# Fewer, wider warm-up matmuls, and the sort matrices' second half moved ahead of the first scores, in an attention and expert-mixture kernel on one core

## The chip, the core and the metric

The kernel runs on one NeuronCore of one Trainium2 chip. The metric is the device time of one execution in microseconds (us). A profile of one execution stands beside it; its times are counted from the first instruction of the span. Engines are named as in the profile: PE is TensorE (matmuls), PEld its weight loads, DVE is VectorE, ACT is ScalarE, POOL is GpSimd, SP is SyncE (which issues DMAs).

## The reference

Four batches of eight heads, 768 tokens of 64 numbers. Eight blocks of 96 tokens are mixed by an 8x8 matrix per head, which five rounds of row and column normalisation make (a Sinkhorn iteration); then attention within each block; then a mixture of four experts over the 3072 resulting rows of 512.

```
P = sort_net
for _ in range(5):
    P = exp(P - max(P, -1))
    P = P / (sum(P, -1) + 1e-9)
    P = P / (sum(P, -2) + 1e-9)
k_sorted = einsum('bhij,bhjcd->bhicd', P, k_blocks)      # v likewise
scores = q_b @ k_sb.T / sqrt(64)                         # within a block of 96
x = softmax(scores) @ v_sb                               # -> rows [3072, 512]
p = domain_probs / (sum(domain_probs, -1) + 1e-9)
out = sum over e of p[:, e] * (relu(x @ w1[e]) @ w2[e])
```

## The kernel before

The order of the work on each engine is the order in which the program is written: no scheduler moves anything. Four batches follow each other; attention of a later batch is spread in small pieces between the expert matmuls of an earlier one, by a table of slots (`PLANS`). Batch 0 has nothing in front of it, so its attention is written out by hand as a head (lines 1365 to 1417), in half heads of queries and half sets of blocks, and the change lies there and in what comes before it.

Before the head, three things run beside each other. DMAs issued by POOL bring queries, keys, values and then weights (lines 147, 110, 134, 141). ACT and DVE go through the five rounds on the 32 sort matrices (`sn`, lines 283 to 300): an Exp on ACT (L284) and five or six small operations on DVE, each waiting for the last. And PE runs matmuls on a constant tile, whose results nobody reads, by `warm` (L260): 84 of them with a moving operand of 128 columns, then, behind the fifth Exp in the program's text, 48 transposes of the first half of the queries (`h_q`, L271, copied by ACT at L274) and 30 more. PE doesn't wait for the Exp here, but ACT's copies of the transposed queries stand behind it on ACT.

After the fifth round, L304 writes the matrices in fp16, repeated 16 times (`sn16`): the first half of the rows on DVE, the second half on POOL. `r_half(a)` (L316) transposes a half by four matmuls into `ps_R`; for the first half DVE builds from it the operand `PI0` of the mix (L327). `mix_half` (L495) mixes keys or values by matmuls, `mixed` (L506) copies the result out of PSUM (keys to `kT` by ACT, values by DVE), `h_s` (L550) makes scores from `kT` and transposed queries and ACT takes their Exp (L556), `h_w` (L522) transposes mixed values and DVE copies them (L527), `h_a` (L567) multiplies the Exp with the values and DVE divides (L580, L581, tile `xsl`), `h_x` (L598) transposes the result into `xT`, and `group0` (L679) is the first expert layer of expert 0.

The head begins like this; `psm` and `psa` are two pools of two PSUM buffers each, and a buffer is free again when its last reader is done. `ps_R` is one of the two of `psm`; `mk1` takes the buffer that `ps_R` had, and `mv1` is in turn behind `mk1` and `mk0` in that pool.

```
mk0 = mix_half("k", 0, 0, psm, 8)      # 8 matmuls of keep_warm (L481) first
mixed("k", 0, mk0, 0, 2, act)
mv0 = mix_half("v", 0, 0, psa)
mixed("v", 0, mv0, 0, 2, vec)
h_s(0, 0)
r_half(1)
mixed("k", 0, mk0, 2, 2, act)
vec(Rs..., Rv...)                      # L1372: Rs, both halves in fp16
```

`Rs` is read by POOL for the second `PI0` and, later, for the mixes of batches 1 to 3.

## Time and profile before

| | us |
|---|---|
| median of 3 runs | 359.47 |
| lowest, highest | 359.26, 360.56 |
| span of the profiled execution | 357.8 |
| its time outside the span | not listed; the median less the span is 1.67 |
| PE busy | 351.6 of the span |
| DVE, ACT, POOL busy | 276.2, 170.6, 133.6 |

The page gives busy time of each engine, the chain of work that ended last (followed back from the last instruction to what released each), groups of instructions by source line, and DMA queues. Matmuls are pipelined: one of 128 columns lasts 219 or 314 ns in the profile, while the starts of such matmuls are 56 or 107 ns apart, so the distance between starts tells what one costs. A wait is the idle time of an engine before an instruction, put down to what released it; "issue" is idle time in which it waited for nothing that the profile shows.

### The profile page before, as it was taken

The numbers are of one execution on the slowest core, as the hardware profiler recorded it, in microseconds if no ns is written. First come the engines' busy times: TensorE is split into PE (matmuls) and PEld (weight loads), VectorE is DVE, ScalarE is ACT, GpSimd is POOL, SyncE is SP. The second block draws the span as 40 slices with busy tenths as digits, with TensorE's granted clock in tenths as the row PEclk, the third lists the DMA queues.
The fourth block names the chain that finished last, engine by engine and source line by source line (L and its number), as shares of the span: only waits on it lengthen the run. The fifth ranks groups of instructions, "written<-read, shape, count | busy, mean of one in ns | idle before, by whom it ended". The sixth has DMA issues, their size and how long they took to land.

```text
span 357.8 us, 9498 instructions
## 1 busy us (share of the span) xinstructions
PE 351.6 (98%) x3949; PEld 306.3 (86%) x3949; DVE 276.2 (77%) x552; ACT 170.6 (48%) x303; POOL 133.6 (37%) x149
## 2 busy tenths in 40 slices
PE   8899999999999999999999999999999999999996
PEld 8686867888888888888899988888888888888886
DVE  5754797869889587868978988896678886588963
ACT  2554240442434535367947258830288611688201
POOL 8864010375122222000535318840058800188400
PEclk9999999999999999999999999999999999999999
DMA  8999999999999999935996420005200015100011
GB/s 114 207 205 228 216 210 198 209 163 165 201 154 160 188 152 170 194 74 73 168 201 90 102 78 0 2 2 108 102 29 2 3 39 138 61 0 2 2 73 46
DMA packets 72022, 40.51 MB, mean 113 GB/s; under 512 B 40614, under 2 KB 66732, under 8 KB 71980
## 3 DMA queue, kind: packets, MB, share of 16 engines
q0 software_dynamic: 36576, 19.93, 41.9%
q1 hardware_dynamic: 35260, 19.92, 28.5%
q8 instruction: 31, 0.51, 0.6%
q14 instruction: 11, 0.09, 0.1%
q10 hardware_dynamic: 144, 0.07, 0.1%
HBM read 42.13 MB, written 6.34 MB: 135 GB/s over the span
## 4 chain that ended last, share of the span: by engine, by line
PE 95%; DVE 2%; ACT 1%; DMA 0%; issue 0%; DVEq 0%
PE ps_h L790 18%; PE ps_Q L1264 18%; PE ps_p L774 12%; PE ps_X L1121 10%; PE ps_Z L1121 7%; PE ps_Q L1121 7%; PE ps_Z L1264 6%; PE ps_h L679 3%; PE ps_o L714 3%; PE ps_p L830 3%; PE ps_a L453 2%; PE ps_s L418 2%; PE ps_k L399 1%; PE ps_v L365 1%; PE ps_a L567 1%; PE ps_mk L495 1%
## 5 line engine op out<-in xcount | busy, mean ns | idle before, releaser
L790 PE MATMUL ps_h<-xT,w 128*128 128x256 f16 x576 | 67.5, 273 | 0.0
L790 PEld LDWEIGHTS <-w 128*128 128x128 f16 x576 | 55.2, 98 | 7.2
L796 DVE SCALAR_TENSOR_TENSOR Hb<-ps_h,pb 128x1024 f16<-128x1024 f32 x34 | 41.5, 1223 | 17.2 <-PE ps_h L790 15.8
L1121 PEld LDWEIGHTS <-w 128*128 128x128 f16 x480 | 43.6, 98 | 4.8
L1134 POOL TENSOR_TENSOR arena<-tmp,pb 128x512 f16<-128x512 f32 x12 | 15.2, 1275 | 65.7 <-PE ps_Z L1121 49.8
L1264 PEld LDWEIGHTS <-Hb 128*128 128x128 f16 x320 | 31.1, 98 | 3.5
L1133 ACT ACTIVATE tmp<-tmp 128x512 f32<-128x512 f32 x46 | 29.0, 632 | 3.9 <-DVE tmp L1171 3.9
L1264 PEld LDWEIGHTS <-Sb 128*128 128x128 f16 x304 | 28.3, 98 | 3.0
L1121 PEld LDWEIGHTS <-arena 128*128 128x128 f16 x312 | 27.7, 98 | 2.9
L425 ACT ACTIVATE ET<-ps_s 96x768 f16<-96x768 f32 x24 | 18.0, 802 | 25.1 <-PE ps_s L418 24.8
L121 POOL DMA_DIRECT2D arena<-in_q_dram x24 | 19.9, 838 | 25.5 <-DMA q_ring<-arena 25.2
L408 ACT CAST kT<-ps_k 64x384 f16<-64x384 f32 x48 | 22.7, 473 | 13.3 <-PE ps_k L399 12.3
L1121 PE MATMUL ps_X<-ET,arena 128*128 128x256 f16 x168 | 25.2, 272 | 0.0
L1264 PE MATMUL ps_Q<-w,Hb 128*128 128x256 f16 x192 | 24.6, 273 | 0.0
L774 PEld LDWEIGHTS <-Hb 128*128 128x128 f16 x232 | 21.8, 98 | 3.0
L1127 DVE SCALAR_TENSOR_TENSOR Hb<-ps_X,pb 128x512 f16<-128x512 f32 x27 | 18.7, 691 | 7.0 <-PE ps_X L1121 7.0
L1141 ACT COPY ps_X<-ps_Z 128x512 f32<-128x512 f32 x27 | 15.4, 571 | 17.8 <-PE ps_Z L1121 17.8
L1121 PE MATMUL ps_Z<-xT,w 128*128 128x256 f16 (+1 forms) x176 | 22.5, 258 | 0.0
L760 DVE TENSOR_TENSOR Sb<-Hb 128x512 f16<-128x512 f16 x33 | 20.6, 647 | 0.0
L1148 ACT COPY tmp<-ps_X 128x512 f32<-128x512 f32 x26 | 15.2, 585 | 9.2 <-PE ps_X L1121 6.6
L1127 DVE SCALAR_TENSOR_TENSOR Hb<-ps_Z,pb 128x512 f16<-128x512 f32 x27 | 18.4, 682 | 1.3 <-PE ps_Z L1121 1.3
L1171 DVE TENSOR_TENSOR tmp<-ps_Q,tmp 128x512 f32<-128x512 f32 x26 | 17.8, 683 | 0.8 <-PE ps_Q L1121 0.8
(266 smaller groups left out, 741.6 us busy)
## 6 DMA issues: line engine op xcount, KB each, us to landing
w<-in_moe_w_dram POOLq DMA_DIRECT2D x6, 1024.0 KB, 27.9
pb<-p_dram SPq DMA_DIRECT2D x9, 512.0 KB, 7.0
arena<-in_k_dram POOLq DMA_DIRECT2D x8, 384.0 KB, 9.3
arena<-in_v_dram POOLq DMA_DIRECT2D x8, 384.0 KB, 7.5
vs<-arena SPq DMA_DIRECT2D x36, 66.0 KB, 4.9
arena<-in_q_dram POOLq DMA_DIRECT2D x24, 96.0 KB, 7.5
out_dram<-ob SPq DMA_DIRECT2D x9, 256.0 KB, 2.0
w<-in_moe_w_dram POOLq DMA_DIRECT2D x4, 512.0 KB, 12.5
```

Of the source, the lines that this page charges most:

```text
L121: nc.gpsimd.dma_start(t[:, h // 2, :, h % 2, :], q[b, h].rearrange("(t p) d -> p t d", p=P))
L408: nc.scalar.copy(kT[ds(D * hh, D), r], pk[ds(D * r, D), hh].rearrange("p a (i c) -> p a i c", c=CP),)
L425: nc.scalar.activation(ETs[2 * (pr % 2) + hh][:, 0:S].rearrange("c (a x) -> c a x", a=2), pss[hh][0:BLK, :, 0:HS], AF.Exp, bias=0.0, scale ...
L760: tt(sm[0], blk(0, 1), blk(1, 1), ALU.add)
L774: nc.tensor.matmul(ps, lhs(e, f), Ts[e][rhs][:, f, :], start=(first and e == es[0] and f == 0), stop=(done and e == es[-1] and f == KH - 1 ...
L790: nc.tensor.matmul(ps[:, f, :], w1sb[e][:, kc, ds((4 * g + f) * P, P)], xT[:, kc, ds(2 * c * P, 2 * P)], start=(kc == 0), stop=(kc == NKC ...
L796: nc.vector.scalar_tensor_tensor(out=Hb[:, homes.get(e, e), ds(4 * g, 4), :], in0=ps[:], scalar=0.0, op0=ALU.max, in1=weights(e).broadcast ...
L1121: nc.tensor.matmul(dst[:, ds(f * cols, cols)], a[lhs][:, k, ds((f0 + f) * P, P)], t[rhs][:, k, :], start=(first and f == 0 and k == 0), st ...
L1127: nc.vector.scalar_tensor_tensor(out=home(i, j), in0=src.rearrange("p (f x) -> p f x", f=m), scalar=0.0, op0=ALU.max, in1=weight(j).broadc ...
L1133: nc.scalar.activation(src, src, AF.Relu, bias=0.0, scale=1.0)
L1171: tt(t12, Q, u2, ALU.add)
L1264: nc.tensor.matmul(ps, lhs(e, f), Ts[e][rhs][:, f, part], start=(first and e == 0 and f == 0), stop=(e == E - 1 and f == KH - 1), skip_gro ...
```

## The change

The warm-up is split differently: 50 matmuls of 128 columns ahead of the query transposes, and 14 behind them, each with a moving operand of 4 x 128 columns (the constant tile, read four times) that writes a whole PSUM bank. `r_half(1)` moves ahead of `h_s(0, 0)`, and the copy of `Rs` moves from DVE to ACT and directly behind it. On ACT the copy stands between the first key copy and the Exp of `h_s(0, 0)`. PE has 50 matmuls and 50 weight loads fewer; DVE has one instruction less and ACT one more; the order on POOL and SP is the same.

```diff
-    def warm(n):
+    def warm(n, wide=1):
         ps = psM.tile([P, 4, P], F32, tag="ps", name=f"ps_w_{state['n']}")
         state["n"] += 1
         for m in range(n):
-            nc.tensor.matmul(ps[:, m % 4, :], dummy, dummy, start=True, stop=True)
+            nc.tensor.matmul(
+                ps[:, ds(m * wide % 4, wide), :],
+                dummy, dummy.rearrange("p (o x) -> p o x", o=1).broadcast_to([P, wide, P]), start=True, stop=True,
+            )
...
-    warm(84)
+    warm(50)
...
             for qd in range(2):
                 h_q(qd, 0, nc.scalar.copy)
-            warm(30)
+            warm(14, 4)
...
     mixed("v", 0, mv0, 0, 2, vec)
+    r_half(1)
+    act(Rs.rearrange("p g (a i) -> p a g i", a=2), Rv.rearrange("p a i g -> p a g i"))
     h_s(0, 0)
-    r_half(1)
     mixed("k", 0, mk0, 2, 2, act)
-    vec(Rs.rearrange("p g (a i) -> p a g i", a=2), Rv.rearrange("p a i g -> p a g i"))
```

## The prediction

> **What bounds the kernel now.** I read the page first, then who waited for whom on TensorE, then the chain of work and the timeline of the first 30 us, and the DMA view in slices of less than 0.1 us.

> The page, busy times, and the shares of the chain that ended last:

> ```profile
> PE 351.6 (98%) x3949; PEld 306.3 (86%) x3949; DVE 276.2 (77%) x552; ACT 170.6 (48%) x303; POOL 133.6 (37%) x149
> PE 95%; DVE 2%; ACT 1%; DMA 0%; issue 0%; DVEq 0%
> ```

> TensorE is the bound. Its waits over the whole span (in total, times, longest):

> ```profile
> PE ps_w L260 <- DVE Hb L152: 1.1, 1, 1.1
> PE ps_R L316 <- DVE sn L304: 1.0, 1, 1.0
> PE ps_s L522 <- issue: 0.2, 1, 0.2
> PE ps_s L550 <- ACT kT L506: 0.2, 1, 0.2
> PE ps_s L550 <- issue: 0.2, 1, 0.2
> PE ps_mk L495 <- DVE Rs L1372: 0.2, 1, 0.2
> ```

> All of them lie before 20.3 us; after that TensorE never stops for as much as this view lists. So whatever the change brings is what it moves at about 20.5 us, and from there it passes to the end nearly one for one. The change only edits instructions between 1 and 15 us. The chain there (start, us, what):

> ```profile
> 13.78 0.21 PE ps_s L550
> 13.99 0.18 issue
> 14.17 0.33 PE ps_s L550 x7
> 14.50 0.21 PE ps_R L316 x4
> 14.71 0.02 issue
> 14.73 0.43 DVE Rs L1372
> 15.17 0.04 issue
> 15.21 0.57 PE ps_mk L495 x24
> ...
> 20.07 0.20 issue
> 20.27 0.37 PE ps_s L522 x3
> ```

> Two things are to be seen. The second half of the sort matrices (ps_R, then its copy Rs) stands in the chain, because the next mix (ps_mk) needs the PSUM buffer that Rs frees. And twice TensorE stands still for "issue": nothing the profile shows holds it.

> **What "issue" is here.** Counting matmuls in the timeline, the first stop is before the 224th (84+48+30+4+8+48+1 went before), the second 128 later, that is 256 instructions with their weight loads. The page's queue "q8 instruction" moved 31 packets, 0.51 MB: 16.5 KB each, one per 255 TensorE instructions (2 x 3949 / 31). In DMA slices of 11.78 to 11.86 and of 17.85 to 17.92 us there is one such packet, in the slices just before none:

> ```profile
> q8 instruction: 1, 0.02, 73.8%
> ```

> ```profile
> q8 instruction: 1, 0.02, 83.5%
> ```

> Both stops end 2.4 us after a packet's start (14.17 - 11.79, 20.27 - 17.86). The next packets start at 17.86 and 23.89, 3.7 and 3.6 us after the stops end. So I read: crossing a boundary of 256 instructions asks for the block after the next boundary, and it is there 3.65 + 2.4 = 6.05 us later. TensorE stops where it runs 256 instructions in less. The third boundary came at 26.87, its packet at 29.75: 2.9 instead of 3.65, so instructions had been taken in about 0.8 us before TensorE ran them.

> [...]

> **The change, part by part.**

> *Warm-up, 84+30 short to 50 short + 14 wide.* One-microsecond windows of ps_w alone (PE busy, matmuls):

> ```profile
> 5.06:6.06 1.00, 1.00 (x13) 1.00 1.10 129
> 6.06:7.06 1.00, 1.00 (x21) 1.00 1.18 161
> ```

> The trace has starts 107 ns apart until 5.94 us and 56 ns apart from 6.08. Before, the 84 end their issue at 8.04 and the transposes of L271 start at 8.19. After: 47 x 107 + 3 x 56 ns from 1.06, so the transposes start at about 6.3; both query transfers landed by 5.88, so they don't wait. They end at 7.0. Nobody gains: ScalarE copies them only behind the fifth Exp, which waits for VectorE and starts at 9.54. The wide ones: the 128x512 matmuls of L714 stand 216 ns apart, so 14 x 0.216 = 3.0 us, 7.1 to 10.1, against 10.65 before. Both are over before 11.79, when L316 starts on sn16. On the path: 0. The cover is 1.7 us; without it, it would cost one for one.

> *50 matmuls and 50 weight loads fewer ahead of everything.* This shifts the boundaries by 100 instructions. The 223rd matmul is now the last of the first four L522 transposes (50+48+14+4+8+48+4+8+4+24+8+3), near 15.9 us, while its block, asked for by 6.9, is there by 13. First stop gone. The next boundary falls in the L567 group that ran at 23.40 before; asked for at about 15.6, there by 21.7. Second stop gone. The third falls 19 matmuls into the L271 group, 28.35 before. From 23.40 to 28.35 is 4.95 us, under 6.05: a **new stop**. Without the lead it is 1.1 us, with the lead of 0.8 seen above 0.3, with a lead over 1.1 nothing. The matmuls of L679 ahead of it, 82 ns apart, leave more time to take instructions in than before the third boundary, so I take 0.2. Later boundaries have 6.9 us and more between packet and use, against 2.4.

> *r_half(1) ahead of h_s(0,0).* Its four matmuls (0.26 us) need the half of sn16 that POOL ended at 12.65 and VectorE's PI0 builds, ended by 13.0; they go into the hole between 13.40, when the last mix is issued, and 13.78, when kT is copied. Cost 0; if the hole were gone, 0.15. No DMA moves on any queue.

> *Rs copied by ScalarE.* VectorE loses 0.42 us at 14.73. ScalarE's copy of 128x256 isn't in the trace; from its copies of 128x384 (0.48) and 128x768 (0.82) a straight line gives 0.37, bounds 0.15 and 0.48. It waits for r_half (about 13.75), starts behind the kT copy at 13.78 and ends at 14.15 (13.95 to 14.3). Queued behind it on ScalarE are the Exp of L556, then three kT copies. The Exp needs h_s, which without the stop ends its results at 13.78 + 0.35 = 14.13 (the later h_s takes 0.34). So the Exp starts at 14.22 instead of 14.54: 0.3 earlier (0.2 to 0.4).

> *What is late next.* mk1 could go at 14.6 rather than 15.21, since Rs has freed its buffer; but mv1 (16.73) needs the buffer that the last of ScalarE's three kT copies frees (15.25 + 1.43 = 16.68). That chain begins at the Exp, so mv1 gains 0.3, not 0.6. Behind mv1, VectorE's copy (17.34), L522 (17.95) and L567 (18.95) follow it. Where the second stop was, the L598 at 20.47 would wait for xsl, which VectorE ended at 20.32, so the stop's 0.2 is worth 0.05 more. POOL's build from Rs starts at 15.39 because its DMA issues end then, and no weights come sooner.

> Sum: -0.3 - 0.05 + 0.2 = -0.15 us. The profiled execution lists no time beside its span of 357.8; the median of the three runs, 359.47, lies 1.67 above. So span 357.65, time **359.3 us**.

> **Rivals.**

> 1. *The third stop is whole.* For it: the two stops that are seen came with turnarounds of 6.1 us. Against: the lead at the third boundary. -0.35 + 1.1 = +0.75: 360.2.
> 2. *The gain doesn't get through.* ScalarE's copy takes its upper bound, the Exp starts little sooner, and the third stop takes the rest: 359.5 to 359.7.
> 3. *More comes through.* Both stops wholly (0.35 and 0.36 us between starts, over what such matmuls take) and no new one: -0.75: 358.7.
> 4. *Slower: the clock is not up when the wide matmuls start.* Before, 84 matmuls without a break stood ahead of the transposes; 50 leave 0.1 us between 6.03, when the pace changed, and their end. If it changes later in an execution, up to 48 transposes stand in between, and wide ones go at 4 x 107 = 427 ns. They end by 11.79 if at most 8 go so, i.e. if the pace changes by 10.5. If none changes, 7.1 + 14 x 0.427 = 13.1, +1.3 us, and the first work behind it at half pace adds up to about the same again: 361 to 362.2. For it: the small margin. Against: the fast pace came 5 us after the first matmul, and before the deadline there is work for 9 us.

> [...]

> **Chances.** Forecast (359.0 to 359.5) 0.45; rival 1 0.17; rival 2 0.18; rival 3 0.10; rival 4 0.10. 0.5% is 1.8 us, about what a measurement of this kernel can tell from no change. Rival 4's upper half and a little of the unforeseen are slower by more; nothing here gives 1.8 us back, as all the waits above but the first two sum to 0.8. Faster 0.04, same 0.88, slower 0.08. The range takes in rivals 1 to 3: 358.6 to 360.6.

> **What would show it.** (Line numbers of the changed kernel, three higher.) Right: no "issue" before L553's matmuls near 14 us; the L559 Exp at 14.2; mv1 near 16.45; an instruction packet near 26 us and a stop in L274 near 28. Wrong: a stop of 1 us there; ps_w matmuls wide at 427 ns; the four r_half matmuls after 13.8; ScalarE's Rs copy over 0.5 us.

## The result, and the profile after

The changed kernel takes 360.56 us (median of 19 executions, 359.43 to 365.17); the kernel before, on the same chip, 359.83 (19, 359.13 to 360.95). The ratio is 1.0034, with a 95% interval of 1.0017 to 1.0050, so the change makes the kernel slower by about a third of a per cent. One of the 19, at 365.17, is left out of the ratio because the comparison counts it as disturbed. The forecast was 359.3.

The profiled execution of the changed kernel took 364.82, with a span of 363.0 (1.8 between them). It is one of the longest. From its page, busy times, the granted clock in 40 slices of 9.1 us, an instruction queue, and the shares of the chain that ended last:

```profile
PE 352.8 (97%) x3899; PEld 305.4 (84%) x3899; DVE 275.5 (76%) x551; ACT 171.1 (47%) x304; POOL 133.7 (37%) x149
PEclk9789999999999999999999999999999999999999
q14 instruction: 12, 0.10, 0.1%
PE 87%; DMA 9%; DVE 2%; POOL 1%; issue 0%; DVEq 0%; POOLq 0%
```

TensorE's share of the chain fell from 95 to 87%, and DMA, which had 0%, has 9. The clock shows 7 and 8 tenths in the second and third slice. TensorE's waits in the same trace (in total, times, longest, us):

```profile
PE ps_R L319 <- DVE sn L307: 2.3, 1, 2.3
PE ps_h L793 <- DVE Hb L799: 1.7, 1, 1.7
PE ps_w L260 <- DVE Hb L152: 1.1, 1, 1.1
PE ps_o L249 <- DMA T<-p_dram: 1.0, 1, 1.0
PE ps_mv L498 <- DMA arena<-in_v_dram: 0.4, 1, 0.4
```

The two stops named "issue" are gone, as forecast, and so is the wait for Rs. The first line is the hole, the idle time of TensorE behind the shorter warm-up: 2.3 us instead of 1.0. Two waits are new behind 20 us (L249 at 34 us, L793 at 103 us); before, there was none. Stretches of the same trace, TensorE alone (us, PE busy, matmuls, granted clock, DMA share, GB/s):

```profile
12.00:14.37 2.37, 1.95 (x67) 1.00 1.30 209
14.37:21.20 6.83, 6.77 (x117) 0.50 1.18 206
21.20:24.00 2.80, 2.69 (x41) 1.00 1.25 206
```

For 6.83 us the head runs at half the clock. Set matmul by matmul against the trace of before, TensorE is 0.2 us late at 15.2 us (the first half of the values landed at 13.56 us instead of 11.12, the last line of the waits), 1.9 late at 19.3, 2.9 at 31 (after the wait in L249) and 4.8 at 98 (after the wait in L793, for a `pb` that landed at 101.3 instead of 96.3). The chain of that stretch shows how a late head becomes a late transfer (start, us, what):

```profile
21.54 0.69 DVE xsl L584
22.22 0.23 DVE T L237
...
22.48 6.78 DMA p_dram<-T
29.26 0.02 issue
29.28 4.58 DMA T<-p_dram
```

VectorE's pieces of the expert weights stand behind xsl, so the store of `p_dram` leaves at 22.48 instead of 20.58, and the load behind it is what L249 waits for.

So the long head and the late transfers behind it make up this execution's 364.8. They do not explain the median. The mean granted clock, which each execution lists, was 0.995 or less in 6 of the 19; the other 13 have a median of 360.27, still above before. So there are at least two losses, and the theories were, in turn: (1) the clock falls again after the warm-up ends early; rivals: the third fetch stop, and the clock opening late; (2) for executions with the clock up, the new place of the 256-instruction blocks, or a transfer that takes the gain back; (3), formed after twelve runs, one ScalarE instruction more.

### The profile page after: what moved, and what is told of

Its sections match the earlier page's. It is cut to its first block, busy times and chain, and to the rows that moved or that the text cites. A ratio compares the mean times of both kernels' runs of the same rounds, so it can differ in the third digit from the quotient of the medians.

```text
span 363.0 us, 9399 instructions
## 1 busy us (share of the span) xinstructions
PE 352.8 (97%) x3899; PEld 305.4 (84%) x3899; DVE 275.5 (76%) x551; ACT 171.1 (47%) x304; POOL 133.7 (37%) x149
## 4 chain that ended last, share of the span: by engine, by line
PE 87%; DMA 9%; DVE 2%; POOL 1%; issue 0%; DVEq 0%; POOLq 0%
PE ps_Q L1267 17%; PE ps_h L793 17%; PE ps_X L1124 10%; PE ps_p L777 9%; PE ps_Z L1124 7%; PE ps_Q L1124 7%; PE ps_Z L1267 6%; DMA pb<-p_dram 3%; DMA arena<-in_v_dram 3%; PE ps_p L833 3%; PE ps_o L717 2%; DMA p_dram<-T 2%; PE ps_h L682 1%; PE ps_a L456 1%; PE ps_s L421 1%; DMA T<-p_dram 1%
## 5 line engine op out<-in xcount | busy, mean ns | idle before, releaser
L793 PE MATMUL ps_h<-xT,w 128*128 128x256 f16 x576 | 67.5, 273 | 1.7 <-DVE Hb L799 1.7
L793 PEld LDWEIGHTS <-w 128*128 128x128 f16 x576 | 55.2, 98 | 9.0 <-issue 1.9
L799 DVE SCALAR_TENSOR_TENSOR Hb<-ps_h,pb 128x1024 f16<-128x1024 f32 x34 | 41.4, 1223 | 19.3 <-PE ps_h L793 15.8
L1137 POOL TENSOR_TENSOR arena<-tmp,pb 128x512 f16<-128x512 f32 x12 | 15.2, 1276 | 65.7 <-PE ps_Z L1124 49.8
L121 POOL DMA_DIRECT2D arena<-in_q_dram x24 | 19.9, 840 | 20.3 <-DMA q_ring<-arena 20.3
L1124 PE MATMUL ps_Z<-xT,w 128*128 128x256 f16 (+1 forms) x176 | 22.5, 258 | 0.0
L763 DVE TENSOR_TENSOR Sb<-Hb 128x512 f16<-128x512 f16 x33 | 20.5, 645 | 0.0
L1151 ACT COPY tmp<-ps_X 128x512 f32<-128x512 f32 x26 | 15.2, 586 | 9.2 <-PE ps_X L1124 6.6
```

The source lines that it names most:

```text
L121: nc.gpsimd.dma_start(t[:, h // 2, :, h % 2, :], q[b, h].rearrange("(t p) d -> p t d", p=P))
L763: tt(sm[0], blk(0, 1), blk(1, 1), ALU.add)
L793: nc.tensor.matmul(ps[:, f, :], w1sb[e][:, kc, ds((4 * g + f) * P, P)], xT[:, kc, ds(2 * c * P, 2 * P)], start=(kc == 0), stop=(kc == NKC ...
L799: nc.vector.scalar_tensor_tensor(out=Hb[:, homes.get(e, e), ds(4 * g, 4), :], in0=ps[:], scalar=0.0, op0=ALU.max, in1=weights(e).broadcast ...
L1124: nc.tensor.matmul(dst[:, ds(f * cols, cols)], a[lhs][:, k, ds((f0 + f) * P, P)], t[rhs][:, k, :], start=(first and f == 0 and k == 0), st ...
```

## The experiments

Executions of the kernel before ran with each group; medians 359.62, 359.71, 359.55 and 359.38 (35, 29, 29 and 35 executions, 359.12 to 361.49 over all). Ratios are to those of the same group. "Clock low" counts executions with a mean clock of 0.995 or less; 0.995 is what the profiled execution of e1 (below) lists, with one stretch of 3.41 us at half speed.

### The change again, and its two parts

`e0_both` is the change. In `e1_warm_only`, the two head lines are as before. In `e2_order_only`, the warm-up is as before:

```diff
-    warm(50)
+    warm(84)
...
-            warm(14, 4)
+            warm(30)
```

> The changed kernel once more, as the measure for the three others. Theory C (clock): the wide warm-up ends near 9.4 us, TensorE has nothing to do until 11.8, and in part of the executions its clock falls to half for one or two stretches of 3.4 us: most executions near 360, some (one in four) at 362 to 365 with a mean granted clock of 0.99 or less, median 0.5 to 1 us above the kernel before. Theory F (instruction fetch): a third stop of up to 1 us near 28 us in every execution, so all of them are 0.5 to 1 us later and none at 364. Theory O (order): the moved matmuls or the copy on ScalarE hold something up, the same in every execution.

> Only the warm-up is changed (50 short + 14 wide); the head has the order of before, with the copy of Rs on VectorE. Theory C: as the whole change, some executions at 362 to 365 with a clock below 0.995. Theory F: also as the whole change, 0.5 to 1 us later in every execution, since the boundaries shift alike. Theory O: like the kernel before, 359.8.

> Only the order is changed (second half of the sort matrices ahead of the first scores, copy on ScalarE); the warm-up is 84 and 30 short ones. Theory C and theory F: 0 to 0.3 us faster than before, no execution above 361, clock 1.0 throughout; the first stop for instructions stays near 14.1 us. Theory O: 0.5 to 1 us slower.

Measured: both 361.01 us, 1.0043 [1.0018, 1.0068], clock low in 3 of 12; warm-up alone 360.74, 1.0035 [1.0012, 1.0058], 4 of 12; order alone 359.83, 1.0006 [0.9996, 1.0015], 0 of 11. So the falling clock belongs to the warm-up. Theories C and F had expected the order part to be 0 to 0.3 us faster than before, with its first fetch stop in place; it was 0.21 slower, and its profile has no stop. In the profile of the warm-up alone the clock opens at 5.92 and is at half from 12.75 to 16.16 us. (Where the clock opens, the starts of the 128-column matmuls go from 107 to 56 ns apart: at 4.13 us in the long execution of the change, at 5.99 in the profile of before. At half, between 19.75 and 20.07 us of the former, they are 107 ns apart again.)

### How the second part of the warm-up is filled

```diff
-            warm(14, 4)
+            warm(22, 4)          # e3_both_22wide
+            warm(56)             # e5_short_106: 128 columns each
+            warm(14)             # e8_64_short: 14 of 128 columns
```

`e4_114_matmuls` has `warm(84)`, then `warm(22)` and `warm(8, 4)`; `e6_64_filled` has `warm(46)` and `warm(18, 4)`; `e7_14wide_50tiny` is the change with this behind its 14 wide ones, and `e9_114_early_end` has it behind `warm(50)`, with `warm(14, 2)` after the transposes:

```diff
+            for _ in range(50):
+                nc.tensor.matmul(tiny[0:32, 0, 0:8], dummy[:, 0:32], dummy[:, 0:8], start=True, stop=True)
```

> The whole change with 22 wide matmuls in place of 14, so that TensorE is busy until 11.1 to 11.8 us, and 8 x 0.216 = 1.7 us of the idle time are filled. Theory C: no execution above 361.5, mean clock 1.0, time 359.2 to 359.8, or up to 0.5 us more where the last wide one ends behind 11.8. Theory F and theory O: as the whole change, 0.5 to 1 us slower than before.

> The changed order, with a warm-up of 84 short, then 22 short and 8 wide: 114 matmuls as before the change, so the blocks of 256 instructions lie where they lay, and TensorE is busy until 11.0 to 11.9 us. Theory C (the clock falls when the warm-up ends early) and theory A (what is left of the loss in executions at full clock comes from where the blocks of instructions lie) both expect 359.6 to 359.9, no clock below 0.997 and no straggler above 361. A theory by which wide matmuls do harm by themselves expects 360 and stragglers.

> The whole change with 56 short matmuls in place of the 14 wide ones: the same columns, the same end near 9.5 us, no wide one, and 106 matmuls in all, 8 from before. Theory C: the clock is at 0.995 or less in about 3 of 10 executions, which take 361 to 365, since only the early end counts. Theory A: in executions at full clock 359.6 to 359.9 and no stragglers. If wide matmuls are what the clock gate dislikes, no clock below 0.997.

> The whole change with 46 short and 18 wide matmuls: 64 in all as in the change, so the blocks of instructions lie as there, but TensorE is busy until 10.2 to 10.9 us as in the kernel before. Theory C: at most one execution with a clock of 0.995 or less. Theory A: executions at full clock stay at 360.0 to 360.4 as in the change, with one or two stragglers of 361.3 to 364 in twelve. If the loss is the clock's alone: 359.6 to 359.9 and no straggler.

> The whole change with 50 matmuls of 32 weight columns and 8 moving columns behind the 14 wide ones: 114 in all, blocks of instructions as before the change, TensorE occupied until 10.8 or so, but by little work. Theory A: executions at full clock go back to 359.6 to 359.9, no stragglers. Theory C: depends on what the clock gate takes for activity; if these count, no clock below 0.997, if they don't, 0.995 or less in about 3 of 10.

> The change with its 14 matmuls behind the transposes back to 128 columns: 50 + 14 short ones, so the warm-up ends its issue near 7.9 us and TensorE has nothing to do for 3.9 us before the transposes of the sort matrices (2.4 us in the change). Theory 1, it is the end of the work before its time that lets the clock fall again: a mean clock of 0.995 or less in at least a third of the executions (30% with the 14 wide ones), a half-speed stretch of 3.4 us or more between 10 and 22 us in a profile that catches it, and a median of 360.8 us or more. Rival 1a, the wide matmuls themselves let it fall (56 short ones with the same end did not, in 11 executions): no execution below 0.998, 360.0 to 360.4. Rival 1b, the place of the instruction blocks alone makes the rest of the loss (64 matmuls ahead of the head, as in the change and in 46 + 18 wide): executions over 361.5 us at full clock, median 360.3 to 361.

> The change with 114 matmuls again, as before it, but still with an early end: 50 tiny ones (32 x 8) directly behind the 50 short ones, and the 14 behind the transposes with 2 x 128 columns instead of 4 x 128. They should end their issue near 9.3 us (9.4 in the change). With the 50 tiny ones behind the wide ones the time was 359.70, no execution below 0.998. Theory 1, the early end lets the clock fall: 0.995 or less in about 3 of 10 executions, and a tail to 362 or more; median 360.2 or more. Rival 1b, the place of the instruction blocks decides: 359.6 to 359.9 as in the two other kernels with 114 (359.83, 359.70) and no execution over 361, with the clock up.

Measured, by the hole that TensorE has in the profile before the transposes of `sn16` (L316; with its range where several profiles fall into a row):

| warm-up | hole, us | clock low | median, us, ratio |
|---|---|---|---|
| as before (before and five kernels here) | 0.9 to 1.9 | 3 of 185 | |
| 50 + 22 wide (e3) | 0.3 | 0 of 12 | 360.05, 1.0029 [1.0009, 1.0050] |
| 84 + 22 + 8 wide (e4) | 0.6 | 1 of 11 | 360.45, 1.0028 [1.0013, 1.0043] |
| 50 + 14 wide + 50 tiny (e7, e15) | 0.7, none | 0 of 24 | e7: 359.70, 1.0007 [0.9996, 1.0019] |
| 50 + 56 short (e5) | 1.0 | 0 of 11 | 360.07, 1.0016 [1.0002, 1.0030] |
| 46 + 18 wide (e6) | 1.2 | 0 of 8 | 361.33, 1.0054 [1.0028, 1.0080] |
| the change's (after, e0, e1, e14) | 1.6 to 2.3 | 13 of 55 | |
| 50 + 50 tiny + 14 of 256 (e9) | 2.7 | 6 of 12 | 360.37, 1.0031 [1.0016, 1.0047] |
| 50 + 14 short (e8) | 4.4 | 4 of 4 | 364.33, 1.0138 [1.0123, 1.0153] |

With more of the hole filled (e3, e4, e6, e7, e15) the clock fell in 1 of 55 executions, with the change's warm-up in 13 of 55, with 2.7 us in half, with 4.4 us in all. But most rows rest on one profile, and the hole of one kernel varies with the moment at which the clock opens. So e5's 1.0 comes from the latest opening of all, 7.02 us: from the first transpose to the end of the warm-up it takes 4.27 us, the changed kernel 4.15, so with an equal opening its hole would be only 0.1 us shorter than the change's (an estimate from these two profiles). Theory C expected 3 falls in 10 there, and none in 11 came. And the old warm-up had holes of up to 1.9 us with 3 falls in 185. So a longer hole makes a fall likelier, but the length at which that begins is not shown. Wide matmuls alone are not it (e3, e6, e7 have them; e8, without, is worst). The stretches of e8, TensorE alone:

```profile
6.00:9.00 3.00, 1.36 (x50) 1.00 1.21 178
9.00:11.41 2.41, 0.00 (x0) 1.00 1.30 201
11.41:14.80 3.39, 3.01 (x70) 0.50 1.28 207
...
21.66:25.00 3.34, 3.32 (x49) 1.00 1.24 205
```

The warm-up had ended at 7.36. The clock, which had opened at 4.59, falls at 11.41, 6.82 us later, with no matmul in the last 2.41 us, and comes back at 21.66, after 10.25 us. In the two other profiles that caught a fall it came 10.24 us after the opening (the change's long execution, 4.13 to 14.37) and 6.83 (e1, 5.92 to 12.75), and lasted 6.83 and 3.41 us. All six lengths lie within 0.02 us of once, twice or three times 3.41; why is not shown. The clock opened at 3.84 to 7.02 us in the eighteen profiles, so the hole's distance from the opening varies. That this alone decides whether a hole of 2 us makes it fall is not shown: it opened at 4.13 us in the long execution of the change and at 4.18 in the profile of e14 (below), and fell in the first only. There the hole was 2.3 us and not 2.0, and TensorE waited 0.4 us more for the late values. Nor did the fall need an idle TensorE directly ahead of it: in the changed kernel TensorE was idle for 2.3 us in one piece, up to 11.80, and busy for 1.95 of the 2.37 us before the clock fell at 14.37.

With the clock up, e6 still has executions of 361.9 to 363.8, and e3 of 362.4 to 363.2, where theory C had expected none above 361.5. Theory A, the place of the blocks, missed in e4, e5 and e6, which lie above what it gave for them, and hit in e7. Of the kernels with 114 matmuls and the new order, e2, e7 and (clock up) e9 lie at 359.83, 359.70 and 359.62; e4, which also has 114, does not (360.32 with the clock up). So the place of the blocks was neither shown nor refuted by these.

### Does a load of `pb` take the gain back?

```diff
     def load_p(b, c):
+        if (b, c) != (0, 0):
+            return pbs[(0, 0)]
```

`e10_before_one_pb` is the kernel before with this, `e11_order_one_pb` the order part with it. Both leave out seven loads and use the first block's expert weights for the later ones.

> The kernel before, with only the first load of broadcast expert weights (pb); every later pair of row blocks uses the first one's, so the output differs and 7 loads of 0.5 MB are left out. It is the base for the next kernel. Theory 2 (the landing of pb near 96 us takes back what the head gains) and its rival (other transfers take it) both expect 359.0 to 359.8 here, since TensorE had no wait that the profile lists after 20.3 us.

> The order part of the change alone (r_half(1) and the ScalarE copy ahead of the first scores, warm-up as before), again with only the first load of pb. Without this cut it was 359.83 against 359.62 of before, though its profile was 0.47 us ahead until 97.8 us and level afterwards, where it waited for pb. Theory 2, pb takes the gain back: 0.35 to 0.5 us less than the kernel before with one pb. Rival 2a, another transfer or the head itself takes it (the second half of w1 near 21.6 us, or loads after 100 us): within 0.15 us of the kernel before with one pb, and the profile shows at which wait the lead goes.

Measured: 359.26, 0.9991 [0.9980, 1.0001], and 359.69, 1.0009 [1.0001, 1.0018]. Without the loads the order part is not 0.4 us quicker than before but 0.43 slower, so this theory fell. Yet the pair told two things. First, e10 has the order of before and no "issue" stop in its profile, and the Exp of the first scores starts as early as with the new order (ScalarE; start, us). Before's order, here from `e13_before_two_act` below, which has the same head:

```profile
13.25 0.48 ACT L509 CAST kT<-ps_mk 128x384 f16<-128x384 f32 x1 [2.08 <-PE ps_mk L498]
14.17 0.81 ACT L559 ACTIVATE ET<-ps_s 96x768 f16<-96x768 f32 x1 [0.44 <-PE ps_s L553]
```

and the new order, from e2:

```profile
13.24 0.48 ACT L506 CAST kT<-ps_mk 128x384 f16<-128x384 f32 x1 [2.08 <-PE ps_mk L495]
13.82 0.37 ACT L1370 CAST Rs<-ps_R 128x256 f16<-128x256 f32 x1
14.17 0.81 ACT L556 ACTIVATE ET<-ps_s 96x768 f16<-96x768 f32 x1
```

14.17 in both. Of the ten profiles with 114 matmuls only two have the stops, that of before and e11's, where the first packet of TensorE's instructions came latest (11.79 and 11.50 us against 10.1 to 11.2).

Second, all TensorE work of e9 is 0.48 us ahead of before from 20.5 us to the last matmul, and its span is only 0.16 shorter. The rest is lost behind the last matmul.

### One ScalarE instruction more

The page of before has

```profile
q14 instruction: 11, 0.09, 0.1%
```

where the page after has 12. The twelfth packet, 8 KB, lies in the last microseconds. Of the changed kernel, 360 to 363 us (queue, packets, MB, share; then the last output store with its KB and us to landing):

```profile
q14 instruction: 1, 0.01, 1.1%
...
out_dram<-oa SPq DMA_DIRECT2D x1, 64.0 KB, 2.0
```

In the kernel before, no packet of that queue lies between 355 us and the end, and the same store takes

```profile
out_dram<-oa SPq DMA_DIRECT2D x1, 64.0 KB, 1.6
```

In eleven profiles with the copy of Rs on ScalarE the packet starts 1.26 us after the start of the last matmul, and the store that ends the kernel takes 1.93 to 2.20 us; in three without it the packet starts 3.9 to 4.2 us after, when all is written, and the store takes 1.58 to 1.60. In the trace of before, two neighbours in ScalarE's stream go at 0.10 us after that start (when ScalarE has finished its work) and at 2.80 (in the closing exchange of the engines). The packet of the changed kernel comes 1.16 us after the former moment, that of before, at 3.93, 1.13 us after the latter. So the author's estimate, from these times, was that with one more instruction the packet follows an instruction of ScalarE that goes 2.7 us earlier, and starts during the last store. Tested by taking it away and by adding it elsewhere:

```diff
-    act(Rs.rearrange("p g (a i) -> p a g i", a=2), Rv.rearrange("p a i g -> p a g i"))
+    vec(Rs.rearrange("p g (a i) -> p a g i", a=2), Rv.rearrange("p a i g -> p a g i"))
```

in e2 (`e12_order_dve_copy`), in the change (`e14_change_dve_copy`) and in e7 (`e15_tiny_dve_copy`), and in the kernel before (`e13_before_two_act`):

```diff
     warm(84)
+    nobody = const.tile([P, 4], F16, name="nobody")
+    nc.scalar.copy(nobody[:, 0:1], dummy[:, 0:1])
+    nc.scalar.copy(nobody[:, 2:3], dummy[:, 0:1])
```

> The order part alone (r_half(1) and the copy of Rs ahead of the first scores, warm-up as before), but with that copy left on VectorE, so ScalarE has as many instructions as before. Theory 3, the one ScalarE instruction more moves a fetch of 8 KB into the last output store: 11 packets in the second instruction queue instead of 12, the last store takes 1.6 us instead of 1.9 to 2.2, and the time is 0.3 to 0.5 us below the 359.83 of the order part: 359.2 to 359.5, lowest 359.1 to 359.2. Rival 3a, the new order itself costs it, wherever the copy is made: 359.7 to 359.9, lowest 359.5 or more.

> The kernel before with two more ScalarE instructions, copies of one column of the constant tile behind the first warm-up matmuls in the text, which nobody reads and for which nobody waits. Theory 3: 12 packets, the last store takes 1.9 to 2.2 us, 0.3 to 0.5 us over the kernel before, lowest 359.5 or more instead of 359.13. Rival 3a: the same time as the kernel before within 0.1 us.

> The whole change, with the copy of Rs left on VectorE (at its new place). Theory 3: its executions with the clock up are 0.3 to 0.5 us below those of the change, 359.2 to 360, the store takes 1.6 us. The clock still falls in about 3 of 10 executions, which have 361 to 365. Rival 3a: nothing changes, lowest 359.8, median 360.5 to 361.

> The change with 50 tiny matmuls behind the 14 wide ones (359.70, no execution below 0.998) and the copy of Rs left on VectorE. Theory 3: both losses are gone, 359.2 to 359.4, no execution over 361, and at least level with the kernel before, 0 to 0.4 us below its median. Rival 3a: 359.7 as with the copy on ScalarE.

Measured: e12 359.23, 0.9990 [0.9974, 1.0005]; e13 359.93, 1.0003 [0.9986, 1.0021]; e14 360.11, 1.0018 [1.0000, 1.0036], clock low in 0 of 12; e15 359.38, 0.9988 [0.9974, 1.0002]. The intervals are wide, since before itself ran from 359.12 to 361.47 in this group (three executions with the clock low); e13's ratio alone shows no loss. For e14, theory 3 had expected the clock to fall in 3 of 10 and at most 360 us with the clock up; the first missed, the second by 0.11. The profiles are plain. Before with two ScalarE copies, from 354.8 us:

```profile
q14 instruction: 1, 0.01, 1.2%
...
out_dram<-oa SPq DMA_DIRECT2D x1, 64.0 KB, 1.9
```

The order part with the copy on VectorE, from 355.85 us, has no such line, and

```profile
out_dram<-oa SPq DMA_DIRECT2D x1, 64.0 KB, 1.6
```

The lowest times part without overlap: 359.12 to 359.14 in before, e1, e10, e12, e14 and e15, whose ScalarE has no instruction more, and 359.43 to 359.99 in the eleven with more (e8, whose clock always falls, not counted). The medians say +0.60 (e12 to e2), +0.43 (e10 to e11), +0.32 (e15 to e7) and +0.55 (before to e13), the pairs e12/e2 and e15/e7 across groups. From the end of the last matmul to the end of the span it is 3.49 to 3.76 us in the twelve profiles whose ScalarE has more instructions, and 3.15 to 3.19 in the six others. The cause is shown: two copies that nobody reads, at 2 us, lengthen the last store. How the packet and the longer store hang together is not shown; what the profiles show is that the two lie beside each other in time.

## Why the prediction was wrong

Two costs were put at nothing, the early end of the warm-up and the added ScalarE instruction, and a gain of 0.3 us was counted that the kernel before has by itself in some executions. That 360.56 lies within the stated 358.6 to 360.6 is luck: the upper end stood for rival 1, which did not come.

**"-0.3, the Exp starts at 14.22 instead of 14.54".** It starts at 14.17 in the profiles of e0 and e2 (at 14.80 in the long execution, where the values landed late), and the reason given, the vanished fetch stop, was the right one. The mistake is that the profiled execution was taken for the typical one: e10 and e13, whose head is that of before, have no stop and start it at 14.17 too. The new order itself is worth 0.02 us (TensorE 0.37 or 0.38 us ahead of the profile of before at 16.7 us in e13 and e10, which have the old order, and 0.39 in e0 and e2).

**"+0.2, a new third stop".** It didn't come. In e0 the boundary in L274 is crossed at 28.26 with its packet at 25.38; the packet had started 2.1 us after the boundary before was crossed, not 3.65. The turnaround was not a constant; rival 1 fell.

**"On the path: 0. The cover is 1.7 us" (the warm-up).** The spacing was as worked out (14 wide ones 217 ns apart), the issue ended at 9.4 to 10.1 us in four profiles (10.1 in the prediction), the early end had no cost as a delay, and the step failed all the same: the sum asked who waits for the warm-up, and not what the hole behind it does to the clock. The clock fell in 13 of 55 executions with this warm-up; the six of them among the result's 19 took 360.56 to 365.17 us, against a median of 360.27 for the other 13. Rival 4 had the resource right and the mechanism wrong: the clock was never late (open by 7.0 us in every profile, against the 10.5 of its decision point); it closed again.

**The term that was not in the sum.** "ACT one more" stood in the list of instructions, priced at its 0.37 us of duration (measured: 0.37), and not as a place in ScalarE's instruction stream. It costs 0.3 to 0.6 us behind the last matmul in each of the twelve profiles that have it. It is not the whole loss with the clock up: e14 is without it and still 0.73 us above the median of before in its group.

**"From there it passes to the end nearly one for one".** In part. In the profile of e14 it does: 0.47 us ahead at 20.5 us and 0.49 at the end, time 359.16. But the second half of the first expert weights landed at 20.4 to 22.5 us where a head with no stop needs it at 21.2; of the order part with the copy on VectorE, TensorE's waits hold

```profile
PE ps_h L679 <- DMA w<-in_moe_w_dram: 1.3, 2, 1.0
```

and e0 loses 0.4 of its lead there, e2 its 0.5 at 98 us behind `pb`. In ten of the fourteen profiles other than before in which the clock stays up, TensorE loses 0.3 to 3.4 us in all behind 21 us: at 21.7 us, where those weights land (e0, e3, e6, e12), at 31 behind a load from `p_dram` (e7, e11), at 98 behind `pb` (e2, e4, e13), or later, where other transfers land (e3, e4, e5). e9, e10 and e14 lose nothing there, e15 loses 0.2. A view that lists no wait doesn't say how close the next one is.

**What stays open.** With neither low clock nor late store, e14 still lies at 360.11, and e1 at 359.99 in its eight executions with the clock up, against 359.23 and 359.38 with 114 matmuls. Both have 50 matmuls fewer ahead of the head and the early end. For the former speak e6 (361.33, later end), e9 (early end with 114 matmuls, 359.62 with the clock up, level with e7's 359.70) and the packet of TensorE that, with 64 or 72 matmuls, starts between 18.3 and 20.1 us, beside the landing of those expert weights, and not at 16.4 to 17.9; against it e4, slow with 114. What e14's usual execution loses no profile shows: the profiled one, 359.16, is one of its two quickest. A kernel with this place of the blocks, a late end and the copy on VectorE (46 short and 18 wide matmuls, or 50 short and 142 tiny ones) has no measurement.

No version beats before beyond its interval: e12 and e15 (0.9990 and 0.9988) are level with it.

## What to carry to other kernels

Before the cost of an edit is summed, ask whether the profiled execution is typical: a stop of 0.2 us that no dependency explains may be in one execution and not in the next, and then its removal is no gain. Count an added instruction on each engine as a place in that engine's stream as well as a duration, and look which of the kernel's last transfers lie beside the instruction packet that it may move (here a store of 1.6 us, which then took 1.9 to 2.2). A warm-up that ends earlier can cost more than the work it saves, though nobody waits for it: here the shorter one, with holes of 1.6 to 2.3 us, let the clock fall in 13 of 55 executions, the old one, with 0.9 to 1.9 us, in 3 of 185, and one profile of either doesn't tell.
